# One attention kernel's output stores: one DMA of 128 partitions, or three of 80, 44 and 4

## The chip, the cores and the metric

The kernel runs on one core of a Trainium2 chip. The metric is the device time of one execution in microseconds (us). The profile of one execution gives each engine's instructions, the DMA packets and the times at which semaphores change. The core has five engines that are told apart here: PE (TensorE; PEld is its weight load), DVE (VectorE), ACT (ScalarE), POOL (GpSimd) and SP (SyncE, which here only issues DMAs). Data is moved by 16 DMA engines. Every DMA adds 16 to a semaphore when it is through; the trace holds these as 16 single completion marks.

## The reference

q, k and v are bfloat16 tensors with 16 x 32 = 512 heads, 192 queries, 1024 keys and a head size of 128.

```python
def reference(q, k, v):
    scale = q.shape[-1] ** -0.5
    scores = jnp.einsum("bhqd,bhkd->bhqk", q, k) * scale
    p = _softmax(scores, axis=-1)
    return jnp.einsum("bhqk,bhkd->bhqd", p, v)
```

## The kernel before, in words

**Tiling.** The 512 heads are cut into 32 groups of 16 (`G`, `NGR`). A group is 8 pairs of heads (`PPG`). The 2 x 192 = 384 query rows of a pair make three units of 128 rows: A (rows 0 to 127 of the first head), B (rows 64 to 191 of the second) and S (the 64 rows left of each). So a group has 24 units (`UPG`). For each unit TensorE makes the scores in PSUM (`s_ps`), VectorE scales them and takes the row extreme (L332), ScalarE or GpSimd make the exponent or the shifted scores (L373, L207), TensorE transposes them (`pt_ps`), ScalarE copies them out (L384, L386), and TensorE multiplies with V into `o_ps`. VectorE divides by the row sums and writes the output tile `ob` (L355, L357), 384 columns for a pair. `ob` has two buffers, so groups g and g + 2 share one.

**Order on the engines.** Each engine has its order written out by hand for a period of two pairs (`PE_ORDER`, `DVE_ORDER`, `ACT_ORDER`), with primes for work of earlier periods. Four periods are a group.

**Loads and stores.** All of them are issued by SP, in program order, on one queue. K and Q come transposed (`load_kq`, L141 and L145), V comes plain (`load_v`, L152). K, Q and V have two buffers each (`NS`), so the loads of group g + 2 wait on SP until the score products of group g are done (K, Q) and until its V products are done (V). The first group's loads come in three parts (`FIRST`). After that SP runs this loop, in which `loads` is a K transpose, a Q transpose and a V load of one group:

```python
            for g in range(NGR):
                if g + NS < NGR:
                    loads(g + NS)
                for a, b in (LAST if g == NGR - 1 else ((0, PPG),)):
                    stores(g, a, b)
```

So on SP's queue a group's store (L170) follows the V load of a later group and is followed by the next group's K transpose. `stores` waits until VectorE has written the group's output tiles. A store of a group moves 128 partitions of 24 runs of 256 bytes, 768 KB. The last group is stored in four parts (`LAST`).

**Semaphores of the stores.** Each `ob` buffer has one (`sst`). VectorE waits on it before the first output of a group (L353) for the store of two groups earlier, by the count that `store_cnt` gives; SP waits on both at the end (L193).

Of the kernel before, what the change touches and what calls it, by code (L numbers as in the profile page):

```python
# [31 lines left out]


def _attention_kernel(nc, q, k, v, out, G=16, NS=2, NSS=4, NX=4, NPT=5,
                      FIRST=((0, 2), (2, 8), (8, 16)), LAST=((0, 4), (4, 6), (6, 7), (7, 8))):
    B, H, SQ, D = q.shape
    SK = k.shape[2]
    assert D == 128 and SK == 1024 and SQ == 192, (D, SK, SQ)
# [2 lines left out]
    NGR = NH // G  # L41
# [6 lines left out]
    NSO = 2  # L48
# [5 lines left out]
    of = out.rearrange("b h s d -> (b h) s d")  # L54
# [15 lines left out]
    with ExitStack() as es:  # L70
        def sb(name, shape, dt):
            return es.enter_context(nc.sbuf_tensor(name, shape, dt))
# [4 lines left out]
        def sem(name):  # L77
            return es.enter_context(nc.semaphore(name))
# [4 lines left out]
        ob = sb("ob", [128, NSO, PPG, 3, 128], BF16)  # L83
# [14 lines left out]
        svl = [sem("svl%d" % i) for i in range(NS)]  # L98
        sf = [sem("sf%d" % i) for i in range(len(FIRST))]
        sfv = [sem("sfv%d" % i) for i in range(len(FIRST))]  # L100
        sst = [sem("sst%d" % i) for i in range(NSO)]
# [23 lines left out]
            return 16 * (g // NS + 1 - (g % NS == 0))  # L125

        def store_cnt(g):
            return 16 * (g // NSO + 1)

        def wait_x(eng, u):  # L130
            eng.wait_ge(s_xp if shifted(u) else s_xa, x_cnt[u])  # L131
# [4 lines left out]
        @block.sync  # L136
        def _(e):
            def load_kq(g, a, b, sems):
                s = g % NS
                h0 = g * G  # L140
                e.dma_start_transpose(  # L141
                    kt[:, s, :, a * 128:b * 128],
                    kf[h0 + a:h0 + b].rearrange("g (p t) d -> (g p) (t d)", t=KT_TILES),
                ).then_inc(sems[0], 16)
                e.dma_start_transpose(  # L145
                    qt[:, s, a * SQ:b * SQ],
                    qf[h0 + a:h0 + b].rearrange("g r d -> (g r) d"),
                ).then_inc(sems[1], 16)

            def load_v(g, a, b, sm):  # L150
                h0 = g * G
                e.dma_start(  # L152
                    vs[:, g % NS, a:b],
                    vf[h0 + a:h0 + b].rearrange("g (p t) d -> p g t d", t=KT_TILES),
                ).then_inc(sm, 16)

            def loads(g):
                s = g % NS
                last_u = (g - NS + 1) * UPG - 1
                if g >= NS:  # L160
                    e.wait_ge(s_qk, last_u + 1)
                load_kq(g, 0, G, (sxk[s], sxq[s]))
                if g >= NS:
                    e.wait_ge(s_pv, last_u + 1)
                load_v(g, 0, G, svl[s])

            def stores(g, a, b):
                so = g % NSO
                e.wait_ge(s_on, g * PPG + b)
                e.dma_start(  # L170
                    of[g * G + 2 * a:g * G + 2 * b].rearrange("h r d -> (h r) d").rearrange(
                        "(n p) d -> p n d", p=128),
                    ob[:, so, a:b].rearrange("p pg y d -> p (pg y) d"),
                ).then_inc(sst[so], 16)

            n = len(FIRST)
            for i in range(n):
                load_kq(0, *FIRST[i], (sf[i], sf[i]))
                if i > 0:
                    for i2 in range(i if i > 1 else 0, i + 1):  # L180
                        load_v(0, *FIRST[i2], sfv[i2])
            for g in range(1, min(NS, NGR)):
                loads(g)
# [3 lines that stand above are left out]
                for a, b in (LAST if g == NGR - 1 else ((0, PPG),)):  # L187
                    stores(g, a, b)
            for so in range(min(NSO, NGR)):
                n_uses = len(range(so, NGR, NSO))  # L190
                if so == (NGR - 1) % NSO:
                    n_uses += len(LAST) - 1
                e.wait_ge(sst[so], 16 * n_uses)  # L193

        @block.gpsimd
        def _(gp):
# [20 lines left out]
        def _(pe):  # L217
# [19 lines left out]
            def qk(u):  # L237
# [13 lines left out]
                if g == 0:  # L251
                    for i, (h, _) in enumerate(FIRST):
                        if h <= b and i not in seen_kq:
                            seen_kq.add(i)
                            pe.wait_ge(sf[i], 32)
                elif u % UPG == 0:
                    pe.wait_ge(sxq[s], load_cnt(g))
# [27 lines left out]
            def pv(u):  # L285
# [14 lines left out]
                for t in range(KT_TILES):  # L300
                    first = t == 0
                    last = t == KT_TILES - 1
                    for at, rows, x in tiles:
                        w = PTS[:, t, rows]
                        pe.ldweights(w, tile_position=at)  # L305
                        if first and at[1] == 0:
                            if g == 0:
                                for i, (h, _) in enumerate(FIRST):
                                    if h <= b and i not in seen_v:
                                        seen_v.add(i)  # L310
                                        pe.wait_ge(sfv[i], 16)
                            elif u % UPG == 0:
                                pe.wait_ge(svl[s], load_cnt(g))
                            if k3 == 0 and pr >= 2:
                                pe.wait_ge(s_on, pr - 1)
                        ins = product(O[rows, sl, :], w, vs[:, s, x, t, :], at, first, last)
                        if with_rs:
                            ins = product(O[rows, 3, sl: sl + 1], w, ones[:, 0:1], at, False, last)
# [8 lines left out]
        def _(dve):  # L327
# [19 lines left out]
            def outputs(pr):  # L347
                g = pr // PPG
                pg = pr % PPG
                so = g % NSO  # L350
                dve.wait_ge(s_pv, max(pv_cnt[u] for u in pair_units(pr)))
                if pg == 0 and g >= NSO:
                    dve.wait_ge(sst[so], store_cnt(g - NSO))  # L353
                sel = slots_of(pr, True)
                dve.reciprocal(rinv[:, pr % 2, sel], o_ps[pr % 2][:, 3, sel]).then_inc(s_ri, 1)  # L355
                dve.wait_ge(s_ri, 2 * pr + 2)
                dve.tensor_tensor(  # L357
                    ob[:, so, pg],
                    o_ps[pr % 2][:, 0:3, :],
                    rinv[:, pr % 2, 0:3].unsqueeze(2).to_broadcast([128, 3, 128]),  # L360
                    ALU.mult,
                ).then_inc(s_on, 1)
# [30 lines left out]
def bass_standalone__mha_softmax__near_ridge_kernel(  # L393
    nc: bass.Bass,
    q: bass.AP,
    k: bass.AP,
    v: bass.AP,
    out: bass.AP,
):
    _attention_kernel(nc, q, k, v, out)  # L400
# [28 lines left out]
```

## Time and profile before

| | us |
|---|---|
| median of 3 runs | 1206.89 (1205.75 to 1207.42) |
| profiled execution, its own time | 1203.52 |
| its span, first to last instruction | 1201.8 |
| PE busy in the span | 1123.8 |
| DVE busy | 1089.6 |
| ACT busy | 1083.3 |
| POOL busy | 485.3 |

| DMA, issued by SP | count | KB each | median us from issue to landing |
|---|---|---|---|
| K transpose | 34 | | 30.4 |
| Q transpose | 34 | | 6.1 |
| V load of a whole group | 31 | 4096 | 15.1 |
| store of a whole group | 31 | 768 | 17.1 |

The profiled execution's own time is 1.7 us longer than its span. The mean granted clock of TensorE is 0.99. An engine's busy time is the time in which it executes; a DMA's time to landing runs from the start of its issue on SP to the last of its 16 completion marks. [...] In tables of stretches, the columns are the stretch, its length, the busy time and number of instructions of PE, PEld, DVE, ACT and POOL, then the granted clock, the DMA engines' busy share and the rate in GB/s.

### The profile page before, as it was taken

How to read it: one execution, taken by the hardware profiler on the slowest of the kernel's cores; microseconds unless marked ns; L12 is line 12 of the kernel's file. 1: busy time of each engine (PE TensorE's matmuls, PEld its weight loads, DVE VectorE, ACT ScalarE, POOL GpSimd, SP SyncE). 2: the span in 40 equal slices, each digit the busy share in tenths (PEclk: the TensorE clock that was granted, in tenths of full speed). 3: DMA queues.
4: the chain of work that ended last, by engine and by line, in shares of the span. 5: the costliest groups of instructions: out<-in, count | busy, mean ns of one | idle time of the engine just before them, and what ended most of it. 6: DMA issues, size and time to landing. Idle time of an engine off the chain costs nothing.

```text
span 1201.8 us, 40191 instructions
## 1 busy us (share of the span) xinstructions
PE 1123.8 (94%) x18432; PEld 844.7 (70%) x15360; DVE 1089.6 (91%) x2304; ACT 1083.3 (90%) x1793; POOL 485.3 (40%) x262
## 2 busy tenths in 40 slices
PE   5599999999999999999999999999999899999998
PEld 3477777777677777776776777777776667777776
DVE  5589998999899999999998999999998899989897
ACT  4689998999899999999998999999998899989898
POOL 2234443444343443443434444343443344334343
PEclk9899999999999999999999999999999999999999
DMA  9999999999999999999999999999999999999991
GB/s 238 238 280 293 264 279 263 267 295 265 289 269 254 275 294 289 274 279 251 279 289 268 293 259 259 295 278 288 291 230 264 281 284 288 264 248 295 275 274 41
DMA packets 789893, 321.34 MB, mean 267 GB/s; under 512 B 724176, under 2 KB 724176, under 8 KB 789712
## 3 DMA queue, kind: packets, MB, share of 16 engines
q1 hardware_dynamic: 789712, 318.78, 111.9%
q8 instruction: 132, 2.16, 0.7%
q14 instruction: 49, 0.40, 0.1%
HBM read 134.22 MB, written 25.17 MB: 133 GB/s over the span
## 4 chain that ended last, share of the span: by engine, by line
PE 51%; DMA 34%; SPq 14%; issue 1%; ACT 1%; DVE 0%; DVEq 0%
DMA vs<-in_v_dram 34%; PE o_ps L220 18%; PE pt_ps L220 17%; PE s_ps L220 16%; SPq L145 8%; SPq L141 5%; ACT x_sb L373 0%; DVE ss L332 0%; SPq L152 0%; ACT pt_sb L384 0%; ACT pt_sb L386 0%; DVE ob L357 0%; DVE rinv L355 0%; DVEq L131 0%
## 5 line engine op out<-in xcount | busy, mean ns | idle before, releaser
L332 DVE TENSOR_SCALAR_CACHE_REDUCE ss<-s_ps 128x1024 f32<-128x1024 f32 x768 | 920.8, 1220 | 95.8 <-PE s_ps L220 77.1
L207 POOL TENSOR_TENSOR x_sb<-ss,nb 128x1024 bf16<-128x1024 f32 x256 | 484.6, 1893 | 704.5 <-DVE ss L332 689.0
L305 PEld LDWEIGHTS <-pt_sb 128*128 128x128 bf16 (+1 forms) x8192 | 442.0, 104 | 238.0 <-issue 140.4
L373 ACT ACTIVATE x_sb<-ss,nb 128x1024 bf16<-128x1024 f32 x512 | 585.4, 1145 | 12.7 <-DVE ss L332 12.7
L220 PE MATMUL o_ps<-vs,pt_sb 128*128 128x128 bf16 (+1 forms) x8192 | 495.9, 219 | 38.6 <-DMA vs<-in_v_dram 38.5
L220 PE MATMUL s_ps<-kt,qt 128*128 128x512 bf16 (+1 forms) x2048 | 466.2, 386 | 35.0 <-DMA qt<-in_q_dram 33.5
L220 PE MATMUL pt_ps<-ident,x_sb 128*128 128x128 bf16 x6144 | 451.3, 220 | 1.3 <-ACT pt_sb L384 1.3
L279 PEld LDWEIGHTS <-x_sb 128*128 128x128 bf16 x6144 | 366.2, 98 | 62.5 <-issue 62.1
L386 ACT ACTIVATE pt_sb<-pt_ps 128x512 f32<-128x512 f32 x512 | 306.0, 598 | 78.6 <-PE pt_ps L220 78.4
L384 ACT ACTIVATE pt_sb<-pt_ps 128x1024 bf16<-128x1024 bf16 x256 | 260.1, 1016 | 21.9 <-PE pt_ps L220 21.9
L220 PE MATMUL o_ps<-ones,pt_sb 128*128 128x1 bf16 x2048 | 189.3, 165 | 0.0
L357 DVE TENSOR_TENSOR ob<-o_ps,rinv 128x384 bf16<-128x384 f32 x256 | 142.7, 557 | 8.8
L263 PEld LDWEIGHTS <-qt 128*128 128x128 bf16 (+1 forms) x1024 | 79.3, 103 | 53.3 <-DMA qt<-in_q_dram 30.5
L373 ACT ACTIVATION_READ_ACCUMULATOR x_sb<-ss,nb 128x1 f32 x512 | 100.7, 197 | 0.0
L332 DVE DVE_READ_ACCUMULATOR ss<-s_ps 128x1 f32 x768 | 63.7, 83 | 0.0
L355 DVE RECIPROCAL rinv<-o_ps 128x1 f32<-128x1 f32 x256 | 41.7, 163 | 4.3 <-PE o_ps L220 4.3
L345 DVE RECIPROCAL rinv<-rs 128x2 f32<-128x2 f32 x256 | 40.9, 160 | 1.1 <-ACT x_sb L373 1.1
L373 ACT ACT_TABLE_LOAD x1 | 1.3, 1283 | 0.8 <-PEq L414 0.8
L199 POOL TENSOR_SCALAR_AFFINE_SELECT ident<-ones 128x128 bf16<-128x128 bf16 x1 | 0.3, 292 | 0.1
L197 POOL MEMSET ones<- 128x128 bf16 x1 | 0.2, 204 | 0.3 <-POOLq L414 0.3
L414 POOL MEMSET const-float32-0.0<- 128x1 f32 x1 | 0.1, 98 | 0.3 <-issue 0.3
L414 POOL MEMSET const-bfloat16-1.0<- 128x1 bf16 x1 | 0.1, 101 | 0.0
(2 smaller groups left out, 0.2 us busy)
## 6 DMA issues: line engine op xcount, KB each, us to landing
vs<-in_v_dram SPq DMA_DIRECT2D x31, 4096.0 KB, 15.1
out_dram<-ob SPq DMA_DIRECT2D x31, 768.0 KB, 17.1
vs<-in_v_dram SPq DMA_DIRECT2D x1, 2048.0 KB, 10.4
vs<-in_v_dram SPq DMA_DIRECT2D x1, 1536.0 KB, 8.4
kt<-in_k_dram SPq DMA_TRANSPOSE x34, 30.4
qt<-in_q_dram SPq DMA_TRANSPOSE x34, 6.1
vs<-in_v_dram SPq DMA_DIRECT2D x1, 512.0 KB, 4.4
out_dram<-ob SPq DMA_DIRECT2D x1, 384.0 KB, 3.2
```

The lines of the kernel that those rows point to most:

```text
L141: e.dma_start_transpose(kt[:, s, :, a * 128:b * 128], kf[h0 + a:h0 + b].rearrange("g (p t) d -> (g p) (t d)", t=KT_TILES),).then_inc(sems[ ...
L145: e.dma_start_transpose(qt[:, s, a * SQ:b * SQ], qf[h0 + a:h0 + b].rearrange("g r d -> (g r) d"),).then_inc(sems[1], 16)
L207: gp.tensor_tensor(x_sb[:, u % NX, :], ss[:, u % NSS, :], nb[:, u % NSS: u % NSS + 1].to_broadcast([128, SK]), ALU.subtract,).then_inc(s_x ...
L220: return pe.add_instruction(mybir.InstMatmult(name=nc.get_next_instruction_name(), engine=mybir.EngineType.PE, ins=[pe.lower_ap(x), pe.low ...
L263: pe.ldweights(w, tile_position=at)
L279: pe.ldweights(w, is_transpose=True, tile_position=(0, 0))
L305: pe.ldweights(w, tile_position=at)
L332: dve.tensor_scalar(ss[:, u % NSS, :], s_ps[u % 2][:].rearrange("p t k -> p (t k)"), -scale, None, ALU.mult, ALU.min, accum_out=nb[:, u % ...
L357: dve.tensor_tensor(ob[:, so, pg], o_ps[pr % 2][:, 0:3, :], rinv[:, pr % 2, 0:3].unsqueeze(2).to_broadcast([128, 3, 128]), ALU.mult,).then ...
L373: act.activation(x_sb[:, u % NX, :], ss[:, u % NSS, :], ACT_FN.Exp, bias=nb[:, u % NSS: u % NSS + 1], scale=-1.0, accum_out=rs[:, pr % NRS ...
L384: act.activation(pt_sb[:, u % NPT], pt_ps[u % 2][:], ACT_FN.Exp, scale=-1.0).then_inc(s_ev, 1)
L386: act.activation(words(pt_sb[:, u % NPT]), words(pt_ps[u % 2][:]), ACT_FN.Copy).then_inc(s_ev, 1)
```

## The change

The store of each group but the last goes as three DMAs, over partitions 0 to 79, 80 to 123 and 124 to 127. They are issued one after the other from the same place on SP's queue. The counts that are waited for on the stores' semaphores are adapted: a store of the first 31 groups now adds 48.

```diff
+                      STORE_PARTS=((0, 80), (80, 124), (124, 128))):
...
         def store_cnt(g):
-            return 16 * (g // NSO + 1)
+            return 16 * len(STORE_PARTS) * (g // NSO + 1)
...
-                e.dma_start(
-                    of[g * G + 2 * a:g * G + 2 * b].rearrange("h r d -> (h r) d").rearrange(
-                        "(n p) d -> p n d", p=128),
-                    ob[:, so, a:b].rearrange("p pg y d -> p (pg y) d"),
-                ).then_inc(sst[so], 16)
+                rows = of[g * G + 2 * a:g * G + 2 * b].rearrange("h r d -> (h r) d").rearrange(
+                    "(n p) d -> p n d", p=128)
+                for lo, hi in (((0, 128),) if g == NGR - 1 else STORE_PARTS):
+                    e.dma_start(
+                        rows[lo:hi],
+                        ob[lo:hi, so, a:b].rearrange("p pg y d -> p (pg y) d"),
+                    ).then_inc(sst[so], 16)
...
             for so in range(min(NSO, NGR)):
-                n_uses = len(range(so, NGR, NSO))
+                n = len(range(so, NGR - 1, NSO)) * len(STORE_PARTS)
                 if so == (NGR - 1) % NSO:
-                    n_uses += len(LAST) - 1
-                e.wait_ge(sst[so], 16 * n_uses)
+                    n += len(LAST)
+                e.wait_ge(sst[so], 16 * n)
```

More of the change, by code (lines that the diff above doesn't have):

```diff
@@ L34, in _attention_kernel @@
 def _attention_kernel(nc, q, k, v, out, G=16, NS=2, NSS=4, NX=4, NPT=5,
-                      FIRST=((0, 2), (2, 8), (8, 16)), LAST=((0, 4), (4, 6), (6, 7), (7, 8))):
+                      FIRST=((0, 2), (2, 8), (8, 16)), LAST=((0, 4), (4, 6), (6, 7), (7, 8)),
+                      STORE_PARTS=((0, 80), (80, 124), (124, 128))):
     B, H, SQ, D = q.shape
```

## The prediction

> **What bounds the kernel now.** I read the page first, then the waits of TensorE, the timeline of SP's queue, and the table of short stretches. TensorE looks like the bound, but the waits say what it is late for:
>
> ```profile
> PE 1123.8 (94%) x18432; PEld 844.7 (70%) x15360; DVE 1089.6 (91%) x2304; ACT 1083.3 (90%) x1793; POOL 485.3 (40%) x262
> ...
> DMA  9999999999999999999999999999999999999991
> ...
> vs<-in_v_dram SPq DMA_DIRECT2D x31, 4096.0 KB, 15.1
> out_dram<-ob SPq DMA_DIRECT2D x31, 768.0 KB, 17.1
> ```
>
> ```profile
> PE o_ps L220 <- DMA vs<-in_v_dram: 38.5, 27, 2.8
> PE s_ps L220 <- DMA qt<-in_q_dram: 33.5, 12, 12.0
> ```
>
> The DMA digits are 9 in all slices but the last. TensorE waits 38.5 us for V in 27 of the 31 later groups, and 33.5 us for Q, of which 12.0 is the start. So 38.5 + 21.5 = 60 us, about 1.9 us a group, are waits for loads. In the chain of waits one pair of heads repeats every 8.63 us twice over (four steps of 8.63 = 34.5 us a group) where nothing is late; the starts of the groups' first score products lie (1156.2 - 59.8) / 30 = 36.5 us apart. The loop that sets the period is therefore the DMA stream. SP's queue shows that stream, always in the same order:
>
> ```profile
> 162.66 4.11 SPq L145 DMA_TRANSPOSE qt<-in_q_dram  x1
> 166.81 0.58 SPq L152 DMA_DIRECT2D vs<-in_v_dram  x1
> 167.44 4.41 SPq L170 DMA_DIRECT2D out_dram<-ob  x1
> 171.89 26.57 SPq L141 DMA_TRANSPOSE kt<-in_k_dram  x1
> 198.50 3.96 SPq L145 DMA_TRANSPOSE qt<-in_q_dram  x1
> ```
>
> The store stands behind V and ahead of the next K transpose. What it costs is read from stretches around its end (columns after the busy times: granted clock, DMA share, GB/s):
>
> ```profile
> 181.00:182.00 1.00, 0.00 (x0) 0.00 (x0) 0.56 (x1) 0.76 (x2) 0.48 (x1) 0.95 1.26 280
> 182.00:183.00 1.00, 0.58 (x9) 0.53 (x4) 0.00 (x0) 0.00 (x0) 0.00 (x0) 0.50 0.89 201
> 183.00:184.00 1.00, 1.00 (x16) 1.00 (x11) 0.00 (x0) 0.00 (x0) 0.00 (x0) 0.50 0.41 96
> 184.00:185.00 1.00, 1.00 (x7) 0.48 (x5) 0.00 (x0) 0.47 (x1) 0.00 (x0) 0.50 1.22 223
> 185.00:186.00 1.00, 1.00 (x15) 0.86 (x14) 0.61 (x1) 0.55 (x1) 0.00 (x0) 0.84 1.28 290
> ```
>
> There is a hole of 1 to 2 us between store and transpose: 96 GB/s against 290. The trace's completion marks (16 for each DMA) name its cause. In this group V's marks run from 180.15 to 182.37 us, the store's from 182.68 to 184.65: one of 16 DMA engines is 2 us behind the others, and the transpose reaches 290 GB/s only when that engine is through. Over the 29 stores that have a K transpose behind them, the last V mark is 1.79 us after the first on average, the last store mark 4.50 us after V's first, and the 1600th transpose packet starts 0.7 to 0.9 us after the store's last mark in most groups, whether that mark is at 4.13 or at 5.41. So the transpose needs all 16 engines in step. A second sign: TensorE's instruction fetches (132 packets of 16 KB) take one engine for about 1 us, and a fetch at 193.79, inside a K transpose, stops the whole stream:
>
> ```profile
> 193.50:194.00 0.50, 0.50 (x7) 0.23 (x4) 0.47 (x4) 0.50 (x2) 0.50 (x1) 1.00 1.39 315
> 194.00:194.50 0.50, 0.50 (x13) 0.50 (x11) 0.50 (x2) 0.50 (x2) 0.37 (x1) 1.00 4.50 143
> 194.50:195.00 0.50, 0.50 (x10) 0.33 (x7) 0.50 (x1) 0.50 (x3) 0.00 (x0) 1.00 0.01 1
> 195.00:195.50 0.50, 0.50 (x8) 0.38 (x7) 0.50 (x1) 0.50 (x2) 0.00 (x0) 1.00 0.08 9
> ```
>
> During V and the store the engines are independent, and there the fetching engine falls behind instead. The slowest engine's share of the store is on the path, once a group.
>
> **The change part by part.** *Bytes and packets:* nothing removed or added; a store stays 3072 packets of 256 B, 24 a partition. *Shares:* now each engine has 8 partitions, 192 packets. From V's first mark to the store's first mark is 2.54 us, 13.3 ns a packet, so 0.32 us a partition. I assume that a DMA of n partitions is dealt in equal runs to the first k engines, k the largest number up to 16 that divides n. The traces of before show this only for n = 128. Then 80 gives 5 partitions to all 16, 44 gives 4 to the first 11, 4 gives 1 to the first 4: 10 for engines 0 to 3, 9 for 4 to 10, 5 for 11 to 15. Times: +0.64, +0.32 and -0.96 us.
>
> [...]
>
> *Which engine is late* the packets do not say, but its place can be worked out. On the small store issued at 1192.44 a fetch falls at 1194.16; 15 marks land within 0.21 us and the 16th 1.81 us after the first. Its packets, 28 ns apart, lead back to a first packet at 1193.460; the other engines' first packets begin between 1193.347 and 1193.450. It is started last or last but one, and in the row of completions of the like store at 1198.04 the missing place is the 15th of 16. If engines are started in the order of their numbers, it is 14 or 15: one that is relieved.
>
> *New end of the store*, from V's first mark: the late engine 4.50 - 0.96 = 3.54. The other engines end at their V lag + 2.57 + 0.64 or 0.32. Their median lag is 0.26 (3.47 at most), but the second-last V mark has 0.96 on average; wherever that engine is, it ends at 4.17 (4 chances in 15), 3.85 (7) or, relieved too, 3.54 at the late engine (4): 3.85 on average. The gain is 0.65; since the lags vary by group and the latest counts, I take 0.6. Bounds: 0.4 (the second engine mostly on a loaded queue) and 0.96 (no other engine interferes). 29 x 0.6 = 17.4 us; bounds 12 and 28.
>
> *SP:* 62 more DMA issues. One costs 0.37 us (the smallest store, all room free) to 0.58 us (V's row), so 0.7 to 1.2 us a group on SP. [...] What is queued behind, K's transpose, isn't needed by the engines until the store ends, 12 us later. I cost this at 0; without the cover it is 29 x 1.2 = 34 us.
>
> *Waits:* VectorE's wait at L353 for the store of two groups earlier now needs 48 counts a store. Behind it stand the first pair's output and the next row maxima. In before, that output starts 2.0 to 5.1 us after the store's last mark; the last mark comes earlier, so nothing.
>
> *Passing on:* K, Q and V behind the store move by the same amount, since the stream has no other gap. TensorE's 34.5 us a group lie below 36.5 - 0.6, so the gain passes 1:1, and V stays the late one, by 1.3 us a group instead of 1.9 for both loads. The last group's stores are unchanged.
>
> The sum: 1203.5 us (the profiled execution: span 1201.8, and 1.7 around it) - 17.4 = 1186.1. That execution was 3.4 us under the median of 1206.9, so on the median 1189.5, which I give.
>
> **The rivals.** *Slower: the late engine gets more, not less.* If the engine of the fetches is among 4 to 10, its end moves by +0.32 us, 29 x 0.32 = +9 us: 1216; among 0 to 3 by +0.64: 1226. It decides from one condition: that engine's number is under 11. For it: the trace holds no numbers. Against: the order of starts and completions above.
>
> *Slower: 44 is dealt to few engines.* If it went to 4 (all powers of two, say), these would hold 5 + 11 + 1 = 17 partitions, ending at 0.26 + 2.57 + 9 x 0.32 = 5.7 against 4.50: +1.2 x 29 = 1243. Break-even lies at 8 + (4.50 - 2.83) / 0.32, some 13 partitions on one engine.
>
> *No change: partitions stay tied to their engines*, whichever DMA carries them. Then every share is 8 again: 1207. Nothing in before excludes it.
>
> *Slower: each DMA has a fixed cost in the stream.* By the smallest store, 1.8 us from issue to landing, two more would be 3.6 x 29 = +104: 1311. Against: the store's first mark is 2.54 us behind V's, all of it taken by 192 packets, so DMAs follow one another without a gap.
>
> [...]
>
> *Slower: SP is late* with K, +34: 1241.
>
> **How the numbers follow.** Forecast 0.70, its own range 1179 to 1195. Late engine on a loaded queue 0.12. Few engines 0.05. Tied partitions 0.07. Fixed cost 0.03, SP late 0.03. A measurement of this kernel tells about 0.2% (2.4 us) from no change. Faster is the forecast, 0.70; same is the tied case and a gain lost on the way, 0.08; slower the rest, 0.22. The range reaches down to 1175: full relief (28 us) and part of the half-clock stretches saved (182 to 185 us above shows 0.50 after TensorE stood still; three such of 3.4 us lose some 5 us). It reaches up to 1216, over the tied case and the milder slower one.
>
> **What would show it.** Right: the last of the three pieces' marks at about 3.9 us after V's first mark instead of 4.50; the hole (96 GB/s) shorter by some 0.6 us; waits for V and Q down from 60 to about 43 us; busy times unchanged; K's issue on SP shorter by what the store's issues grow. Wrong: the store's last mark later than 4.50 (shares or place of the late engine misjudged), or earlier without a shorter period (transposes not gated by it, or a new wait on SP or at L353).

## The result, and the profile after

| | before | after |
|---|---|---|
| median of 6 runs each, us | 1206.89 (1205.52 to 1209.66) | 1226.6 (1218.32 to 1229.91) |
| profiled execution, us | 1203.52 | 1218.32 |
| its span, us | 1201.8 | 1216.6 |
| mean granted clock of TensorE | 0.990 | 0.981 |

The ratio of after to before, estimated from all runs, is 1.0154, 95% interval 1.0133 to 1.0175 (the two medians alone give 1.0163): 1.5% slower, where 1189.5 us was forecast, 1.4% faster. Rivals that end slower had 0.22 in all. The page of after first, its busy times and the DMA issues of the stores:

```profile
PE 1130.8 (93%) x18432; PEld 849.5 (70%) x15360; DVE 1089.9 (90%) x2304; ACT 1083.6 (89%) x1793; POOL 485.3 (40%) x262
...
out_dram<-ob SPq DMA_DIRECT2D x31, 480.0 KB
out_dram<-ob SPq DMA_DIRECT2D x31, 264.0 KB
out_dram<-ob SPq DMA_DIRECT2D x31, 24.0 KB
```

The three pieces are there, 768 KB together. TensorE executes the same 18432 matmuls and is busy 7.0 us longer. The waits of TensorE (total, count, longest, in us):

```profile
PE s_ps L223 <- DMA qt<-in_q_dram: 48.4, 19, 10.9
PE o_ps L223 <- DMA vs<-in_v_dram: 32.0, 23, 2.7
```

They were 33.5 and 38.5 in before: together 80.4 against 72.0. So the span's 14.8 us are 8.4 us of longer waits for loads and 7.0 us of slower matmuls, within 0.6. The matmuls are slower because the clock is lower: the granted clock stands at 0.5 for 47.3 us in all, against 25.2. TensorE is busy for 36.0 us inside these stretches against 15.8 in before, and 13.3 us less than in before outside them, so the 7.0 us lie there. After the first 60 us and but for the end there are seven such stretches of 3.4 or 6.8 us against three of 3.4, and each begins within 1.3 us of a wait of TensorE of 1.9 to 3.2 us; not every wait of that length has one. So I take the second part for a consequence of the first, and ask why the loads are late. The stretches behind a V load (columns as in the first such table, clock, DMA share and GB/s last), here behind a V whose first completion mark is at 180.47, as it was at 180.15 in before:

```profile
182.00:183.00 1.00, 0.98 (x22) 0.92 (x14) 0.00 (x0) 0.14 (x2) 0.00 (x0) 1.00 0.90 196
183.00:184.00 1.00, 1.00 (x16) 0.71 (x13) 0.26 (x1) 0.69 (x1) 0.00 (x0) 1.00 0.50 106
184.00:185.00 1.00, 1.00 (x16) 0.71 (x13) 0.98 (x2) 0.70 (x2) 0.00 (x0) 1.00 0.53 111
185.00:186.00 1.00, 1.00 (x19) 0.86 (x16) 0.93 (x1) 0.27 (x2) 0.00 (x0) 1.00 1.14 243
186.00:187.00 1.00, 1.00 (x30) 0.80 (x28) 0.86 (x4) 1.00 (x2) 0.62 (x1) 1.00 1.28 291
```

The hole between store and K transpose should have become shorter by 0.6 us. It is wider: two rows, 183 to 185, lie near 110 GB/s where before had one (96), between the same 196 to 201 ahead of them and the rise behind. SP's queue says what changed ahead of it (start, duration, instruction):

```profile
163.17 4.01 SPq L146 DMA_TRANSPOSE qt<-in_q_dram  x1
167.23 0.58 SPq L153 DMA_DIRECT2D vs<-in_v_dram  x1
167.86 15.29 SPq L174 DMA_DIRECT2D out_dram<-ob  x3
183.19 16.12 SPq L142 DMA_TRANSPOSE kt<-in_k_dram  x1
199.34 4.86 SPq L146 DMA_TRANSPOSE qt<-in_q_dram  x1
```

The store's issue took 4.41 us in before and takes 15.29 here, until 183.15: 2.7 us *after* V's first mark. Over the 29 stores that have a K transpose behind them, SP is through with the store 8.14 us before V's first mark in before; in after it is through with the three pieces at -8.28, +0.74 and +2.17 us. So the prediction's "0.7 to 1.2 us a group on SP" is in truth 10 us, for the same 768 KB, and what comes late is the store's own second and third piece.

### The profile page after: what moved, and what is told of

The parts are those of the page before. It is cut to its first block, busy times and chain, and to the rows that moved or that the text cites. A ratio compares the mean times of both kernels' runs of the same rounds, so it can differ in the third digit from the quotient of the medians.

```text
span 1216.6 us, 40253 instructions
## 1 busy us (share of the span) xinstructions
PE 1130.8 (93%) x18432; PEld 849.5 (70%) x15360; DVE 1089.9 (90%) x2304; ACT 1083.6 (89%) x1793; POOL 485.3 (40%) x262
## 4 chain that ended last, share of the span: by engine, by line
PE 58%; DMA 31%; SPq 9%; ACT 1%; issue 0%; DVE 0%; DVEq 0%
DMA vs<-in_v_dram 29%; PE o_ps L223 21%; PE pt_ps L223 19%; PE s_ps L223 18%; SPq L142 5%; SPq L146 4%; DMA qt<-in_q_dram 2%; ACT x_sb L376 0%; DVE ss L335 0%; SPq L153 0%; ACT pt_sb L387 0%; ACT pt_sb L389 0%; DVE ob L360 0%; DVE rinv L358 0%; DVEq L132 0%
## 5 line engine op out<-in xcount | busy, mean ns | idle before, releaser
L223 PE MATMUL o_ps<-ones,pt_sb 128*128 128x1 bf16 x2048 | 192.5, 167 | 0.0
```

Of the source, the lines that this page charges most:

```text
L223: return pe.add_instruction(mybir.InstMatmult(name=nc.get_next_instruction_name(), engine=mybir.EngineType.PE, ins=[pe.lower_ap(x), pe.low ...
```

## The experiments

All times are given relative to V's first completion mark, as means over those 29 stores in the profiled execution. **Handed over** means the end of a piece's issue on SP. "Last mark" is the store's last completion mark, "period" the time from group to group, between the last marks of their Q transposes. Each ratio is to before, in runs on the same chip, with its 95% interval.

What I came to: **the more partitions, up to seven, an engine has ahead of the last piece, the later that piece is handed over (-6.60 us with one ahead, 2.14 with seven); its packets come later still; where the engines have run out of the first piece by then, the stream has a gap (39 GB/s in 112, 16).** (In before's small store at 1192.44, told of in the prediction, the first packet starts 0.9 us after the issue does.) Its rivals: each DMA costs a fixed time in the stream (D in the expectations); SP can hold only one DMA behind V, whichever it is (A); the K transpose is handed over too late (K). S and H in the expectations are the accounts whose times the runs mostly bore out: the late last piece, and the order of the pieces on SP. The room in the queues, by which H explains the late handing over, is a guess of mine that no record shows.

**Same pieces, other shares.** All these are edits of one line of after, `STORE_PARTS`.

```diff
-((0, 80), (80, 124), (124, 128))     # after: 80, 44, 4
+((0, 80), (80, 112), (112, 128))     # e1_three_equal: 80, 32, 16
+((0, 112), (112, 128))               # e2_two_equal: 112, 16
+((0, 126), (126, 128))               # e3_two_126_2: 126, 2
+((0, 120), (120, 128))               # e4_two_120_8: 120, 8
```

> Three pieces of 80, 32 and 16 partitions: each piece divides by 16, so that every DMA engine has 5 + 2 + 1 = 8 partitions, as before the change. Only the number of DMAs is that of the change. Theory A (SP takes the pieces late, so that the end of the store and the next K transpose come late; the number of DMAs counts): the store's three issues take some 14 us on SP as with the change (14.7), K is issued about 2 us after V's first completion mark, and the time is 1.0 to 2.0% over before. Theory B (the shares of 10, 9 and 5 partitions put the late engine on a loaded queue): shares are equal, so within 0.3% of before, store's last mark near 4.50 us after V's first. Theory C (pieces dealt to 11 and 4 engines are slow in themselves): as B, within 0.3%.

> Two pieces of 112 and 16 partitions: 7 + 1 = 8 for every engine. Theory A: one piece less to take, so K's issue is about 1 to 2 us earlier than with the three, half or less of the loss: 0.2 to 0.9% over before. Theories B and C: within 0.3% of before.

> Two pieces of 126 (14 engines, 9 each) and 2 partitions (2 engines, 1 each): two engines, by my reading the ones started last, have no share of the store at all, two have 10, the rest 9. Against the two equal pieces: if the late engine is one of the last two, the store's last mark falls to about 3.8 to 4.2 us after V's first and the time lies 0.5 to 1.3% under the two equal pieces; if it is elsewhere, 0.5 to 1.0% over them (Theory B).

> Two pieces of 120 (15 engines, 8 each) and 8 partitions (8 engines, 1 each): only the engine started last is free of the store, eight have 9, seven have 8. Against 126 and 2 it tells the place of the late engine: if it is the last one, as fast as 126 and 2 or up to 0.5% faster; if it is the last but one, it keeps 8 partitions and the time is that of the two equal pieces, within 0.4%.

| | ratio | store's issues on SP, us | last piece handed over | last mark | period |
|---|---|---|---|---|---|
| before | 1 | 4.61 | -8.14 | 4.50 | 36.55 |
| after | 1.0154 [1.0133, 1.0175] | 14.75 | 2.17 | 5.10 | 37.10 |
| 80, 32, 16 | 1.0216 [1.0192, 1.0240] | 14.97 | 2.37 | 5.30 | 37.53 |
| 112, 16 | 1.0139 [1.0109, 1.0168] | 14.87 | 2.14 | 4.89 | 37.20 |
| 126, 2 | 1.0051 [1.0034, 1.0068] | 13.92 | 1.33 | 4.80 | 36.85 |
| 120, 8 | 1.0018 [1.0002, 1.0033] | 14.37 | 1.77 | 4.68 | 36.60 |

With 80, 32, 16 every engine should have 5 + 2 + 1 = 8 partitions, as in before (pieces of 112, 64 and 16 go to 16 engines by their packets, below), and still the kernel is 2.2% slower: a split can cost without uneven shares. After, with its uneven shares, is some 0.6% faster than that. With two pieces and equal shares it is still 1.4%, more than the 0.2 to 0.9% that A gave. So neither shares nor the number of pieces carry the loss, and a late last piece is common to all. 126, 2 came out 0.9% under 112, 16, in the size expected, but not by the placement of the late engine that I had in mind (below). In it and in 120, 8 the shares are uneven too, so what is left of the loss there is not the late piece's alone.

**The same pieces in the other order.**

```diff
+((120, 128), (0, 120))               # e5_small_first: 8, 120
+((112, 128), (0, 112))               # e2r_equal_small_first: 16, 112
+((124, 128), (80, 124), (0, 80))     # e10_change_reversed: 4, 44, 80
```

> The two pieces of 120 and 8 partitions in reverse order: 8 first, 120 second, both behind V. Shares as with 120 and 8. Theory A (behind a V load in flight SP takes one more DMA at once, and the next one only when V is nearly through): now the large piece is taken at about V's first completion mark and its packets come some 2 us later, so the engines stand still; the store's last mark moves from 4.7 to 6 us or more after V's first, and the time is 2.5 to 5% over before. Theory D (each further DMA costs a fixed time in the DMA stream, whatever the order): as with 120 first, 0 to 0.5% over before.

> The two equal pieces in reverse order: 16 partitions (1 for each engine) first, 112 (7 for each) second. Same DMAs, same shares as with 112 first, which cost 1.4%; only the order differs. Theory H (SP hands a DMA on only when the one before it is wholly in the engines' queues, for which room comes as V drains; so a large piece ahead of another DMA holds that DMA and the K transpose up, a small one does not): both issues take some 5 to 7 us on SP instead of 14.9, K's issue begins 6 to 7 us ahead of V's first mark, and the time is within 0.4% of before. If the number of DMAs or their shares cost the time: 1.0 to 1.4% over before as with 112 first.

> The change's own pieces in reverse order: 4, 44, 80. Same DMAs and shares as the change (10, 9 and 5). Theory H: the 4 are handed on at once, but the 44 are 4 partitions, 96 packets, on each of 11 engines and fill the room, so that the 80 and K come late by less than with the change: K's issue begins between 6 us ahead of and 1 us behind V's first mark, and the time lies between 0.8% under and 1.2% over before, in any case 0.4% or more under the change. If the order does not matter for these pieces: 1.3 to 1.9% over before.

Measured: 8, 120 at 0.9985 [0.9970, 1.0001]; 16, 112 at 1.0002 [0.9988, 1.0015]; 4, 44, 80 at 1.0087 [1.0072, 1.0101]. The pair 112, 16 and 16, 112 is the cleanest comparison of the study: same DMAs, same shares, 1.39% against nothing. And 8, 120 speaks against rival A, by which the large piece would have been the late one, at a cost of 2.5 to 5%. SP's queue in 112, 16:

```profile
313.12 0.58 SPq L153 DMA_DIRECT2D vs<-in_v_dram  x1
313.75 15.73 SPq L174 DMA_DIRECT2D out_dram<-ob  x2
329.52 18.84 SPq L142 DMA_TRANSPOSE kt<-in_k_dram  x1
```

and in 16, 112:

```profile
307.02 0.58 SPq L153 DMA_DIRECT2D vs<-in_v_dram  x1
307.64 6.84 SPq L174 DMA_DIRECT2D out_dram<-ob  x2
314.53 25.52 SPq L142 DMA_TRANSPOSE kt<-in_k_dram  x1
```

The two issues together take 15.73 us in the one and 6.84 in the other. Within the 15.73, the small piece's issue alone takes 10.82 us. What follows in the stream, in 112, 16, from 1.5 us after V's first mark (327.65):

```profile
329.15:329.65 0.50, 0.47 (x12) 0.41 (x6) 0.50 (x1) 0.50 (x1) 0.44 (x1) 1.00 0.98 220
329.65:330.15 0.50, 0.50 (x14) 0.50 (x10) 0.02 (x1) 0.22 (x2) 0.00 (x0) 1.00 0.20 39
330.15:330.65 0.50, 0.50 (x8) 0.27 (x4) 0.00 (x0) 0.18 (x1) 0.00 (x0) 1.00 0.71 98
330.65:331.15 0.50, 0.50 (x10) 0.44 (x8) 0.24 (x1) 0.50 (x1) 0.00 (x0) 1.00 0.78 113
331.15:331.65 0.50, 0.50 (x12) 0.49 (x9) 0.50 (x1) 0.35 (x1) 0.00 (x0) 1.00 1.11 196
```

and in 16, 112, from the same point behind its own V (320.24):

```profile
321.74:322.24 0.50, 0.33 (x8) 0.23 (x3) 0.43 (x2) 0.50 (x3) 0.48 (x1) 1.00 1.27 290
322.24:322.74 0.50, 0.50 (x17) 0.50 (x9) 0.50 (x1) 0.50 (x3) 0.50 (x1) 1.00 1.09 246
322.74:323.24 0.50, 0.50 (x10) 0.35 (x7) 0.47 (x4) 0.50 (x2) 0.50 (x1) 1.00 0.33 74
323.24:323.74 0.50, 0.50 (x7) 0.36 (x6) 0.50 (x2) 0.50 (x2) 0.41 (x1) 1.00 0.63 146
```

In 16, 112 the stream runs at 246 to 290 GB/s until 2.5 us and only then comes the hole that before has too. In 112, 16 the rate drops half a microsecond earlier, to 39: seven partitions of the first piece last 7 x 0.32 = 2.2 us behind V, and the eighth, handed over at 1.83 us in this group, isn't there yet. The rate is back at 196 some 1.7 us after the handing over. The mean over the 29 stores, counted from the packets of 256 B in the trace (GB/s in steps of half a microsecond from V's first mark, and KB moved from 1 to 7 us):

```
              0.0 0.5 1.0 1.5 2.0 2.5 3.0 3.5 4.0 4.5 5.0 5.5 6.0 6.5   KB 1-7
before        250 266 274 284 234  73  91 165 180 238 259 270 271 281   1310
after         253 266 250 179 181 141  94 103 123 174 207 227 267 267   1106
80, 32, 16    242 264 228 103 141 180 147 115 149 180 189 206 249 270   1079
112, 16       251 266 275 265 114  84 103 137 175 191 214 239 262 274   1167
16, 112       242 262 273 283 233  80  95 168 169 236 276 279 280 279   1326
64, 64        244 262 268 279 239  88  89 188 163 252 260 262 266 279   1317
4, 44, 80     175 192 206 228 230 216 149 111 177 169 212 256 247 266   1234
K late alone  245 262 272 283 228  78  94 162 151 240 267 277 269 268   1294
```

Two things are to be read here. First, the gap comes where a first piece of 5, 7 or 8 partitions an engine runs out (1.6, 2.2 and 2.6 us): in after from 1.5 us, in 112, 16 from 2.0. Then everything behind comes later: after moves 204 KB less by 7 us, 0.70 us at 290 GB/s, and its period is 0.55 us longer. In 4, 44, 80 the large piece is last and is handed over at 0.41 us; until its packets come, 4 and 44 can keep 11 engines busy, 11/16 x 290 = 199 GB/s, and the table has 192 and 206. Second, the ones that lose nothing have before's curve.

**K late by itself, and two halves.** The first is before with one wait added on SP behind the store, so that K is handed over only when the V load ahead of it has landed; the second is again one line of after.

```diff
+                if g + NS + 1 < NGR:                      # e11_k_late_alone
+                    e.wait_ge(svl[g % NS], load_cnt(g + NS))
...
+((0, 64), (64, 128))                                      # e13_64_64
```

> The kernel before, with its store in one DMA, and one wait added on SP: after the store, ahead of the next K transpose, for the V load ahead of the store to have landed. That moves K's issue from 8.1 us ahead of V's first mark to about 1.8 us behind it, close to the 2.2 us of the change, and touches nothing else. If K's late handing on is what costs the time (Theory K): 1.0 to 2.0% over before. If it is the last piece of the store that comes late, and K is gated by the end of the store alone (Theory S): within 0.5% of before, since K's issue still lies 2.7 us ahead of the store's last mark.

> Two equal pieces of 64 (4 partitions for each engine, each). By Theory H what counts is how many packets an engine has to take ahead of the last piece: with 1 partition ahead both issues took 6 us on SP and the time was that of before, with 3 (10, 22, 96) 10.1 us and no loss to be seen, with 7 (112, 16) 14.9 us and 1.4%. With 4 ahead: 11 to 13 us, K's issue 0 to 2 us ahead of V's first mark, 0.2 to 0.9% over before. If any second large DMA costs the same, whatever its size: 1.4% or more.

SP's queue with K late alone:

```profile
164.93 0.58 SPq L152 DMA_DIRECT2D vs<-in_v_dram  x1
165.55 4.66 SPq L170 DMA_DIRECT2D out_dram<-ob  x1
180.18 16.41 SPq L141 DMA_TRANSPOSE kt<-in_k_dram  x1
```

K's issue starts at +1.86 us instead of -8.1, and the ratio is 0.9996 [0.9985, 1.0007]: no cost. So the prediction's sentence that K isn't needed until the store ends was right, and K is not the victim, at least up to 1.86 us; in 112, 16 it is issued at 2.20 us, and whether the last 0.34 us count was not tried. 64, 64 hands its second piece over at -0.62 us: 1.0001 [0.9988, 1.0014], no cost, where 0.2 to 0.9% was expected. In the queue one sees that its issues still take long:

```profile
165.26 0.59 SPq L153 DMA_DIRECT2D vs<-in_v_dram  x1
165.89 11.73 SPq L174 DMA_DIRECT2D out_dram<-ob  x2
177.66 19.10 SPq L142 DMA_TRANSPOSE kt<-in_k_dram  x1
```

The 11.73 us on SP cost nothing here, where the last piece is handed over at -0.62 us and the first one runs out 4 x 0.32 = 1.3 us behind V. This also speaks against D, a fixed cost per DMA. Equal halves gain nothing and cost nothing, and by 16, 112 and 112, 16 it is the order that decides.

**Another place for the small piece.** Once on SP between K and Q of the next loads, and once on ScalarE's queue.

```diff
-            def load_kq(g, a, b, sems):                   # e6_small_after_k (120 and 8)
+            def load_kq(g, a, b, sems, between=None):     # e6c_equal_after_k (112 and 16)
...
+                if between is not None:
+                    e.wait_ge(s_on, (between + 1) * PPG)
+                    store_part(between, 0, PPG, *STORE_PARTS[1])
...
+                if u >= UPG and u % UPG == 13:            # e7_small_on_act (120 and 8)
+                    small_store(u // UPG - 1)
```

> The piece of 8 partitions is issued earlier: between the K and the Q transpose that stand ahead of the same V load; behind V stands the piece of 120 alone. Shares as with 120 and 8. Theory A: K is issued some 8 us ahead of V's first mark again, as in before; the late engine's relief is kept (1.2% between 120 and 8 and the two equal pieces), and up to 0.5 us a group may be lost between K and Q: 1.4% under before to equal to it. Theory D: two DMAs as before, 0 to 0.4% over before.

> The same place for the small piece, but pieces of 112 and 16 partitions, so that all engines have equal shares and nothing is relieved. Theory A: the 1.4% that the two equal pieces cost behind V are gone, within 0.5% of before. Theory D: 1.4% over before, since the number of DMAs and the shares are the same.

> The piece of 8 partitions is issued by ScalarE, on its own DMA queue, in the third period of the next group; behind V stands the piece of 120 alone. Theory A: K is issued as early as in before and nothing stands between K and Q either: 0.4 to 1.5% under before, unless ScalarE loses over 0.5 us at each issue. Theory D: 0 to 0.4% over before.

Measured: 1.0075 [1.0056, 1.0093], 1.0075 [1.0054, 1.0096] and 1.0030 [1.0016, 1.0043]. All three missed: I had expected next to nothing, or a gain, since no late piece stands behind V any more. Only the third lies in the range that D gave for it (0 to 0.4%), and 64, 64 speaks against D. Between K and Q, a piece costs 0.75% whatever the shares. From K's last mark to Q's takes 3.52 and 3.77 us in the two, against 3.09 in before: with the plain store between them, the two transposes lie 0.43 and 0.68 us further apart. With 112 and 16, K's last mark comes 0.39 us sooner behind V's first than in before, and the break takes 0.68 us; the difference over 29 groups is 8.4 us, close to the 0.75% (9 us). On ScalarE's queue, V's first mark to K's last takes 22.75 us against 22.38.

**The late engine.** With the small pieces first, the shares can be tried without the late piece. They are reckoned here as the prediction does it, with the engines of a smaller piece among those of a larger one; the packets carry no engine numbers, and the times of nine and of ten partitions on one engine, below, fit it.

```diff
+((118, 128), (96, 118), (0, 96))     # e8_relief_small_first: 10, 22, 96
+((117, 128), (0, 117))               # e9_relief_13: 11, 117
```

> Three pieces, small ones first: 10 (1 each for engines 0 to 9), 22 (2 each for engines 0 to 10), then 96 (6 for all). Shares 9, 8 and, for engines 11 to 15, 6. By the completion marks of the change and of 126 and 2, the late engine is one of 11 to 13, so it is relieved by 2 partitions, 0.64 us. If the late engine's end gates the next K transpose and Theory H holds for small pieces up to 3 partitions an engine: 0.3 to 1.3% under before. If the end of the late engine does not gate K (as the piece on ScalarE's queue and 8 ahead of 120 may suggest, though there it was not relieved): within 0.4% of before. If three DMAs hold SP up in this order too: 0.5 to 1.5% over.

> Two pieces, small one first: 11 (1 each for engines 0 to 10), then 117 (9 each for engines 0 to 12). Engines 13 to 15 have nothing of the store, 11 and 12 have 9, 0 to 10 have 10. This places the late engine among 11, 12 and 13. If it is 13, no engine's mark is late, the store's last mark is at 3.9 us after V's first or less, and the time is 0.5 to 1.5% under before if the late engine gates K. If it is 11 or 12, it has one partition more than before: last mark near 4.8, time 0.2 to 1.0% over before.

10, 22, 96 gives ten engines nine partitions, one eight, and five six. It is *faster* than before: 0.9954 [0.9941, 0.9966], 1197.07 us against 1202.1, and it is the version that beats both kernels. Its store's last mark is at 4.44 us. Its waits of TensorE, against 33.5 and 38.5:

```profile
PE s_ps L223 <- DMA qt<-in_q_dram: 30.9, 11, 10.1
PE o_ps L223 <- DMA vs<-in_v_dram: 30.5, 23, 2.5
```

11, 117 gives eleven engines ten, two nine, and three nothing. It is slower, 1.0060 [1.0043, 1.0078], last mark 4.91. With 126, 2 two engines carry nothing and the last mark is late too (4.80). So in most stores the late engine is not one that carries nothing.

Nor is it one engine. In the trace a store has a packet of 4 B for each engine that takes part, 16 in before and 31 in after (16 + 11 + 4). The start of a store's last such packet, counted from V's last mark, I take as the measure of how many partitions the late engine had: with eight on every engine the median is 2.22 us in before and 2.23 in 64, 64 and in 16, 112, and 27, 27 and 26 of the 29 stores lie between 2.15 and 2.35. In 10, 22, 96 it falls apart. In 13 stores it is 1.53 to 1.85 us, as for six partitions (2.22 - 2 x 0.32 = 1.58), in 10 it is 2.50 to 2.70, as for nine (2.54), and from the seventh store on the two kinds mostly alternate. In 11, 117 it is some 2.9 us in 17 stores and some 2.6 in 7, as for ten and nine. So in some stores the late engine is one of the five with six partitions and is relieved; in others it is one of the ten with nine and gets more. This is inferred from the shares and the marks.

## Why the prediction was wrong

**The step that failed** is SP's: "I cost this at 0". The price of one issue was taken from two rows (0.37 and 0.58 us), while in the same rows the issue that stands right behind the store, K's, takes 26.57 us. The prediction didn't ask what the *second piece* of the store finds when it is issued at K's place. It takes over a part of the long issue: the store's issues take 14.75 us instead of 4.61, K's own 16.12 instead of 26.57 in the group shown, and the last piece comes 10 us later than the store had come. No run shows the 0 that the sum had for SP; in its place stand those 10 us. "What is queued behind, K's transpose" named the wrong instruction. What is queued behind the first piece is the rest of the store, whose packets are needed when the first piece runs out, in after 1.6 us behind V's first mark. The rival *SP is late* had the direction and a time of 1241, but the same wrong victim, and its price (29 x 1.2 us of instruction time) has nothing to do with the 0.55 us a group that the gap costs.

**Shares: right in the numbers of engines.** Three pieces put 465 more small marking packets (4 B) into the trace than one, 31 x (11 + 4): 44 is carried by 11 engines and 4 by 4, as assumed. The other traces fit: 496 = 31 x 16 more for 112, 16 and for 64, 64, 217 = 31 x (15 + 8 - 16) for 8, 120, and 651 = 31 x (10 + 11) for 10, 22, 96. A store of after has 33 marks, 16 + 12 + 5, one more than engines for each of the two smaller pieces; in the group shown, a mark comes 0.16 and 0.17 us after their issues end (181.40 after 181.24, 183.31 after 183.14), and in 10, 22, 96 each of the two small pieces has one 0.1 to 0.2 us after its own. Where only 11 engines can work, the rate is that of 11 (192 to 206 GB/s, above). That the pieces take the first engines by number, as the prediction assumed, no trace shows.

**Which engine is late: wrong.** The prediction put it at 14 or 15, always relieved. Already in the group that it shows, two of the store's marks come last, 4.48 and 4.50 us behind V's first, and not one. By 10, 22, 96 it changes from store to store: in some it is one of the five with six partitions, which have five in after, in others one of the ten with nine, which have nine or ten in after. There the rival *the late engine gets more* holds. That it is the engine of the instruction fetches, as the prediction had it, is not shown: in before a fetch of 1.11 us at 68.84 lies inside a V load, and that load's 16 marks still come within 0.18 us (73.35 to 73.53).

**The gain of 0.6 us a group: mis-sized, even without the loss.** 10, 22, 96 takes two partitions (0.64 us) off five engines and is faster by 5.5 us, 0.19 us a group; by the prediction's way of reckoning, one for one, that is under a third. The alternation accounts for much of it: over the 29 stores the last small packet comes only 0.11 us sooner behind V's last mark than in before, since what one store gains the next loses. For the shares of after, with half of the stores relieved by 0.6 us and half loaded by 0.32, I estimate (0.6 - 0.32) / 2 x 29 = some 4 us instead of 17.4. After is some 7.5 us faster than 80, 32, 16 (1.0216 to 1.0154), but its second piece also comes earlier (0.74 against 1.57 us), so not all of that need be the shares.

**The marks.** Last mark at 3.9 us: 5.10. Hole shorter by 0.6 us: wider. Waits from 60 to 43 us: up by 8.4. Busy times unchanged: PE +7.0 us by the clock. K's issue shorter by what the store's grow: as said. (The time of the rival *44 is dealt to few engines* adds up to 1242, not 1243, which changes nothing.) The sentence "Wrong: the store's last mark later than 4.50" was the one that came true. Of the causes in its brackets the place of the late engine was misjudged, but by 80, 32, 16, where all shares are equal and the mark is at 5.30, the late pieces make it late without that.

**What the runs showed in its place.** The time at which the last piece is handed over rises with the partitions an engine has to take ahead of it, up to seven: 1 ahead -6.60 us (8, 120), -6.46 (11, 117) and -5.98 (16, 112), 3 ahead -2.32 (10, 22, 96), 4 ahead -0.62 (64, 64), 5 ahead 0.41 (4, 44, 80), 7 ahead 2.14 (112, 16) and 2.37 (80, 32, 16). Beyond that it rises no further: 8 ahead 1.77 (120, 8), 9 ahead 1.33 (126, 2) and 2.17 (after). Where all shares are equal, nothing is lost up to -0.62 us, and 1.4 and 2.2% at 2.14 and 2.37. In the other kernels the shares differ as well: 11, 117 loses 0.6% by its shares alone, and the 0.5% of 126, 2 can be its shares too, since most of its stores end as with nine partitions on the late engine.

**Still open.** Why a piece is handed over later the more an engine has ahead of it is not shown: no record names what an issue on SP waits for, and the row stops rising at seven. 120, 8 is handed over late (1.77 us) and loses only 0.18%; there only 8 engines have a part of the second piece (the 217 packets of 8, 120, above). Which engines are late, and why they change from store to store, is not known; in 10, 22, 96 the rate still lies between 123 and 181 GB/s from 2.5 to 4.5 us behind V's first mark.

## What to carry to other kernels

When a DMA is cut in pieces, reckon for each piece where on its queue it will be *issued*, not only how many bytes and engines it takes: a long issue of one instruction can pass to what takes its place in the queue (here the store's issue went from 4.41 us to 15.29 and K's from 26.57 to 16.12). A long issue on SP cost nothing by itself (11.73 us in 64, 64); it cost where the engines finished what they had before the next piece came, so in a stream like this put small pieces first, and few enough of them that the large one comes early (16, 112 at no cost, 112, 16 at 1.4%; but 4, 44, 80 at 0.9%). To test such a thing, reverse the order: same DMAs, same shares, another answer. And before relieving the engine that ends last, see over many stores whether it is always the same one; the prediction placed it by two small stores at the end of before.

## What the runs showed of the hardware that was not expected

- An issue of a small store behind a large one took 10.82 us on SP (112, 16); the whole pair took 6.84 us in the other order.
- From the handing over of a piece to the return of the rate took some 1.7 us in the group shown.
- The engine that ends last changes from store to store: in 10, 22, 96 it had six partitions' time in 13 of 29 stores and nine partitions' time in 10.
- A plain store between two DMA transposes lengthened the way from K's last mark to Q's from 3.09 to 3.52 and 3.77 us, for 96 KB or less.
- A kernel with 8.4 us more of waiting lost 7.0 us more in matmul time, through stretches of 3.4 or 6.8 us at a granted clock of 0.5.
